# Where the last spectral outputs and the last stores stand in a fused S4D convolution and gated linear unit

## The chip, the cores and the metric

The kernel runs on one core of a Trainium2 chip. The metric is device time in microseconds of one execution; lower is better. Three runs of the kernel before gave 732.49, 735.47 and 735.87 us, median 735.47 us.

The core's engines are named as in the profile: PE (TensorE, matmuls; PEld is its weight load), DVE (VectorE), ACT (ScalarE), POOL (GpSimd) and SP (SyncE). SP, ACT and POOL also issue DMAs; SPq and ACTq are their queues. SBUF and PSUM are on-chip memories of 128 partitions; matmul results land in PSUM.

## The reference

One sequence of 2048 tokens with 448 channels is normalised and goes through two branches, whose sum with the input is the output. Branch A is a long convolution by FFT with a kernel made from state-space parameters, branch B a gated linear unit with 1792 hidden units. All is in float32.

```python
def _A_ref(u, log_A_real, A_imag, C_real, C_imag, log_dt, D_skip):
    ...
    K = 2.0 * jnp.einsum("dn,dnl->dl", C, P).real
    Kf = jnp.fft.rfft(K, L2)
    Uf = jnp.fft.rfft(u_t, L2)
    y = jnp.fft.irfft(Uf * Kf[None, :, :], L2)[:, :, :L]
    ...
    return y + u * D_skip[None, None, :]

def _B_ref(x, w_gate, w_up, w_down):
    g = jnp.einsum("bsd,df->bsf", x, w_gate)
    u = jnp.einsum("bsd,df->bsf", x, w_up)
    h = _sigmoid(g) * u
    return jnp.einsum("bsf,fd->bsd", h, w_down)

xn = _layernorm(x, axis=-1)
return x + _A_ref(xn, ...) + _B_ref(xn, ...)
```

## The kernel before

**Tokens.** The 2048 tokens are 16 blocks of 128. A block's 128 partitions are four groups `g` of 32; four blocks of one tile are four neighbouring tokens, so one partition of a tile [128, 4, 448] holds four rows that are neighbours in DRAM. Four accumulators `accs[0..3]` hold four blocks each. They start as the input x and collect both branches. The first two (blocks 0 to 7) are written to `acc_d` in the middle and come back as the tile `ac`; the last two (blocks 8 to 15) stay in SBUF. Below, `t` is 0 or 1 for `accs[2]` or `accs[3]` and `b` is 0 to 3 for the block in it.

**Two streams of work.** The program is written by two generators, `conv` (branch A) and `glu` (branch B). A planner at the end of the function takes turns between them by the costs that they yield; the order on each engine is then settled by a scheduler, held by `issue_after` (this instruction stands behind that one) and by priorities. The last group of hidden units yields `None` before block (0,1) (L800): from there the planner runs `conv` to its end, and then `glu`.

**The end of `glu`.** For each block the down products (L811) multiply three tiles of hidden units by `w_down`, each as three products of high and low parts, so nine matmuls into one PSUM bank `po`; VectorE adds half of `po` to the accumulator (L816).

**The end of `conv`.** `spectra` goes through the frequencies in 17 steps. In each, `there` (L893) transforms and multiplies, and `back` (L920) makes the inverse's first part into two PSUM banks, which ACT copies to the tile `vt` (L926); four DMAs store `vt` to the DRAM tensor `v_d` (L938), and `turned` (L944) gathers it back transposed into `vp`. `last(h, m)` (L955) makes from `vp` the spectral outputs of channel half `h` for four blocks: 64 matmuls for two calls, and two additions on VectorE for a call (L963). For `m` 0 and 2 these go to `ac`, for 4 and 6 to `accs[2]` and `accs[3]`. `sp_mm`, a one-element list, names the matmul that the following ones must stand behind.

**The stores.** `out(src, b0, h)` (L233 to L240) stores four blocks of one channel half as four DMAs, one for each group, dealt in turn to SP, ACT and POOL by the counter `outs`. `out` of the half `h = 0` of `accs[2]` and `accs[3]` follows their fourth block, that of `h = 1` everything else.

Of the kernel before, what the change touches and what calls it, by code (L numbers as in the profile page):

```python
# [130 lines left out]
def s4d_glu_kernel(ctx, tc, io):  # L131
    nc = tc.nc
# [4 lines left out]
    x_t, out_t = tok(io["A_u"][0]), tok(io["out"][0])  # L137
# [52 lines left out]
    def acc_tile():  # L190
        return pg.tile([128, 4, D], F32, name="acc", bufs=2)
# [37 lines left out]
    accs = [acc_tile() for _ in range(2)]  # L229

    def blocks(t, g, b0, nb):
        return t[g, :, b0 // 8, b0 // 4 % 2, b0 % 4 : b0 % 4 + nb]

    def out(src, b0, h):

        ds = slice(H * h, H * h + H)
        for g in range(4):
            eng = (nc.sync, nc.scalar, nc.gpsimd)[outs[0] % 3]
            outs[0] += 1
            eng.dma_start(blocks(out_t, g, b0, 4)[:, :, ds], src[32 * g : 32 * g + 32, :, ds])  # L240

    def x_load(dst, b0, nb, engs):
        for g in range(4):
            engs[g % len(engs)].dma_start(dst[32 * g : 32 * g + 32], blocks(x_t, g, b0, nb))
# [474 lines left out]
    def glu():  # L719
        for half in range(2):  # L720
# [4 lines left out]
            for fs_ in ORDER[half]:  # L725
# [3 lines left out]
                final = half == 1 and fs_ is ORDER[1][-1]  # L729
# [64 lines left out]
                for t in range(2):  # L794
                    acc = accs[2 * half + t]
                    for b in range(4):
                        if final and (t, b) == (0, 1):

                            yield None
                        if final and (t, b) == (1, 2):  # L800

                            sp_mm[:] = glu_mm
                            for m in (0, 2):
                                lasts[0](1, m)
                        po = psg.tile([128, D], F32, name="po", tag="gu", bufs=4)
                        bs = slice(128 * b, 128 * b + 128)
                        n = 0
                        with tc.issue_after(sp_mm[0].ins) if glu_on else nullcontext():
                            for (hh, hl), (dh, dl) in zip(hs[t], wts):
                                for a_, w_ in ((hh, dh), (hh, dl), (hl, dh)):  # L810
                                    glu_mm[:] = [nc.tensor.matmul(  # L811
                                        po, a_[:, bs], w_, start=(n == 0), stop=(n == 3 * fc - 1)
                                    )]
                                    n += 1
                        with hp(HP):
                            v.scalar_tensor_tensor(  # L816
                                acc[:, b], po, 0.5, acc[:, b], ALU.mult, ALU.add
                            )
                        yield 0.6 * fc
                        if cross and (t, b) in downs:  # L820
                            step(*downs[t, b])
                    if cross:
                        nc.sync.dma_start(acc_d[:, 4 * t : 4 * t + 4], acc)
                    if final:
                        out(acc, 8 + 4 * t, 0)
                if final:
                    sp_mm[:] = glu_mm
                    for m in (4, 6):
                        lasts[0](1, m)
                    for t in range(2):  # L830
                        out(accs[2 + t], 8 + 4 * t, 1)

    def spectra(pf):

# [14 lines left out]
        def work(n, sh, bufs):  # L849
            return spare[n].pop() if spare[n] else pf.tile(sh, F32, name=n, bufs=bufs)  # L850
# [20 lines left out]
        def bank(name):  # L871
            return psc[-1].tile([128, 2, H], F32, name=name, tag="sp", bufs=4)

        def after():
            return tc.issue_after(sp_mm[0].ins)
# [35 lines left out]
        def back(h, k, ys_):  # L911
            vt = work("vt", [128, 2, 2, H], 2)
            bt, n = (t32[:, 1:3], 1) if k == 32 else (bk, 2)
            pvs = [bank("pv") for _ in range(n)]
            with after():
                for j in range(2):
                    for e in range(2):
                        for i in range(n):
                            s = slice(64 * i, 64 * i + 64)
                            mm = nc.tensor.matmul(  # L920
                                pvs[i][:, j], bt[s, e], ys_[j][s, e], start=(e == 0), stop=(e == 1),
                                skip_group_check=True,
                            )
            sp_mm[:] = [mm]
            for i in range(n):
                nc.scalar.copy(vt[:, i], pvs[i])  # L926


            for j in range(2):
                for i in range(n):  # L930
                    k1 = k + 2 * j + i
                    if k == 32:
                        to, fr = v_d[j, 32::64], vt[0:128:2, 0, j]
                    elif k1 == 0:
                        to, fr = v_d[h, 0::64], vt[0:128:2, i, j]
                    else:
                        to, fr = v_d[h, 8 * (k1 % 4) + k1 // 4 :: 32], vt[:, i, j]
                    nc.sync.dma_start(to.rearrange("r w d -> w r d"), fr)  # L938

        def turned(h, k):  # L940
            if h not in vp:
# [4 lines left out]
        def last(h, m):  # L946

            pos = [bank("pv") for _ in range(2)]
            for i in range(2):
                for g in range(4):  # L950
                    for b in range(2):
                        s = slice(64 * b, 64 * b + 64)
                        w = 8 * g + m + i
                        with after():
                            mm = nc.tensor.matmul(  # L955
                                pos[b][32 * g : 32 * g + 32, i], wf[s, w], vp[h][s, w],
                                start=True, stop=True, skip_group_check=True,
                            )
            sp_mm[:] = [mm]
            for b in range(2):  # L960
                q, o, ds = 2 * (m // 4) + b, m % 4, slice(H * h, H * h + H)
                acc = ac[:, 4 * q + o : 4 * q + o + 2, ds] if q < 2 else accs[q][:, o : o + 2, ds]
                v.tensor_tensor(acc, acc, pos[b], ALU.add)  # L963
            if m % 4 == 2 and m < 4:
                for q in range(2):
                    out(ac[:, 4 * q : 4 * q + 4], 4 * q, h)
# [5 lines left out]
        steps = [(h, k) for h in range(2) for k in range(0, 32, 4)]  # L972
# [6 lines left out]
        for n, (h, k) in enumerate(steps):  # L979
# [18 lines left out]
            while len(wait) > 1 and not (due and wait[0][0] == 1):  # L998
                t = wait.pop(0)
# [5 lines left out]
            yield WS  # L1005
        sp_mm[:] = glu_mm
        back(*prev)
        for t in (*wait, prev[:2]):
            turned(*t)
# [92 lines left out]
    lasts, glu_mm, sp_mm, glu_on, outs, x1s, hfs, xls = [], [], [], [], [0], [0], [], []  # L1102
# [7 lines left out]
    while any(g is not None for g in gens):  # L1110
# [3 lines left out]
        i = min(live, key=lambda i: done[i] / total[i])  # L1114
        try:
            w = next(gens[i])
# [31 lines left out]
```

## Time and profile before

| what | value |
|---|---|
| median of three runs | 735.47 us (732.49 to 735.87) |
| the profiled execution | 737.56 us |
| its span, first to last instruction | 735.7 us |
| mean granted TensorE clock | 0.974 |
| DVE, ACT, POOL busy, share of the span | 76%, 57%, 49% |
| HBM read and written | 72.13 MB, 43.84 MB |

A row of the timeline has the start and duration in microseconds, the engine, the line, the operation with output and input, and how many instructions are merged; in brackets stands the idle time of the engine ahead of it and what ended it. The chain of waits follows the last work back through what released each step. A row `min/median/max` gives the duration of one instruction in nanoseconds, and then when the first and the last started. The rows of GB/s show what the DMA engines moved in 40 equal slices of a window.

### The profile page before, as it was taken

What the parts mean: (1) busy time and instruction counts of PE and PEld (TensorE: products, weight loads), DVE (VectorE), ACT (ScalarE), POOL (GpSimd) and SP (SyncE); (2) the same over time, 40 slices, a digit from 0 to 9 for tenths busy, and PEclk for the clock granted to TensorE, in tenths of its full rate; (3) what the DMA queues carried; (4) which work ended last, traced back from release to release, by engine and by line L of the source; (5) the groups of instructions that cost most, each with busy time, mean ns of one, the idle gap of its engine ahead of it and who ended that gap; (6) DMA issues with size and microseconds to landing.
All of it is one profiled execution on the core that took longest, in us unless ns stands there. A gap on an engine that the chain in (4) does not pass through costs nothing.

```text
span 735.7 us, 19244 instructions
## 1 busy us (share of the span) xinstructions
PE 680.4 (92%) x7780; PEld 535.5 (73%) x7780; DVE 560.1 (76%) x776; ACT 421.1 (57%) x654; POOL 360.6 (49%) x423
## 2 busy tenths in 40 slices
PE   2898699999999898899999999999999999989995
PEld 2676588878877787556778878877877777767783
DVE  5899995779889899778488988977955555555543
ACT  3656275479777778796686787677553322312320
POOL 2101076846987975776365697575943002530001
PEclk9998899999999999899999999999999999989998
DMA  9957155454334445456942332233259999997745
GB/s 205 230 147 205 29 165 158 162 172 151 84 111 153 144 118 163 133 151 190 261 141 83 103 109 89 82 112 98 63 162 302 252 243 255 249 263 161 194 120 157
DMA packets 102984, 117.24 MB, mean 159 GB/s; under 512 B 13232, under 2 KB 90864, under 8 KB 102896
## 3 DMA queue, kind: packets, MB, share of 16 engines
q1 hardware_dynamic: 78736, 91.87, 45.2%
q10 hardware_dynamic: 21584, 18.24, 9.3%
q0 software_dynamic: 2576, 5.90, 3.1%
q8 instruction: 61, 1.00, 0.6%
q14 instruction: 27, 0.22, 0.1%
HBM read 72.13 MB, written 43.84 MB: 158 GB/s over the span
## 4 chain that ended last, share of the span: by engine, by line
PE 63%; DVE 13%; DMA 7%; ACT 7%; issue 4%; SPq 3%; POOL 1%; ACTq 1%; POOLq 0%; DVEq 0%
PE gu L698 29%; PE po L811 11%; PE sp L893 7%; PE ko L605 5%; PE pv L920 4%; PE tr L531 3%; DVE Et L591 2%; DVE Ft L593 2%; DVE Et L592 2%; SPq L633 1%; ACT S L540 1%; ACT S L538 1%; DVE acc L816 1%; SPq L481 1%; DMA t<-in_c_t_dram 1%
## 5 line engine op out<-in xcount | busy, mean ns | idle before, releaser
L509 POOL TENSOR_TENSOR me<-me,pm 128x32 f32<-128x32 f32 (+1 forms) x168 | 140.3, 835 | 107.4 <-DVE Et L592 96.3
L509 POOL TENSOR_TENSOR mf<-mf,pm 128x64 f32<-128x64 f32 (+1 forms) x112 | 118.2, 1056 | 4.7
L698 PE MATMUL gu<-xh,wh 128*128 128x512 f32 x336 | 102.3, 412 | 7.0 <-DVE acc L816 6.1
L698 PE MATMUL gu<-xh,wl 128*128 128x512 f32 x336 | 98.9, 402 | 0.0
L698 PE MATMUL gu<-xl,wh 128*128 128x512 f32 x336 | 97.5, 396 | 0.0
L591 DVE TENSOR_TENSOR Et<-me,S 128x1024 f32<-128x1024 f32 x56 | 82.8, 1479 | 12.5 <-ACT S L540 10.8
L592 DVE TENSOR_TENSOR Et<-me,S 128x1024 f32<-128x1024 f32 x56 | 79.4, 1417 | 12.3 <-ACT me L522 9.6
L811 PE MATMUL po<-dh,hh 128*128 128x448 f32 x224 | 85.0, 380 | 3.9 <-DVE hf L709 3.1
L698 PEld LDWEIGHTS gu<-xh,wh 128*128 128x128 f32 x336 | 63.2, 195 | 28.9 <-DVE acc L816 6.5
L811 PE MATMUL po<-dl,hh 128*128 128x448 f32 x224 | 83.0, 371 | 0.0
L811 PE MATMUL po<-dh,hl 128*128 128x448 f32 x224 | 82.0, 369 | 0.0
L537 ACT ACTIVATE S<-tr 128x1024 f32<-128x1024 f32 x56 | 57.8, 1032 | 41.8 <-PE tr L531 41.2
L593 DVE TENSOR_TENSOR Ft<-mf,S 128x1024 f32<-128x1024 f32 x56 | 76.8, 1372 | 5.2 <-ACT S L540 2.7
L605 PEld LDWEIGHTS ko<-Et,Ft 128*32 128x32 f32 x3584 | 54.1, 110 | 32.8 <-issue 13.2
L605 PE MATMUL ko<-Et,Ft 128*32 128x64 f32 x3584 | 65.0, 221 | 12.3 <-DVE Ft L593 11.4
L698 PEld LDWEIGHTS gu<-xh,wl 128*128 128x128 f32 x336 | 65.1, 194 | 15.2 <-DVE pl L316 0.7
L698 PEld LDWEIGHTS gu<-xl,wh 128*128 128x128 f32 x336 | 64.5, 192 | 14.0
L714 ACT CAST hh<-hf 128x512 fp32r<-128x512 f32 x56 | 34.9, 623 | 64.5 <-DVE hf L709 58.6
L709 DVE SCALAR_TENSOR_TENSOR hf<-th,gu 128x512 f32<-128x512 f32 x56 | 38.1, 681 | 43.6 <-PE gu L698 39.5
L706 ACT ACTIVATE th<-gu 128x512 f32<-128x512 f32 x56 | 33.7, 602 | 64.4 <-PE gu L698 52.0
L540 ACT ACTIVATE S<-S,hpi 128x1024 f32<-128x1024 f32 x56 | 65.6, 1171 | 0.5 <-issue 0.3
L816 DVE SCALAR_TENSOR_TENSOR acc<-po,acc 128x448 f32<-128x448 f32 x80 | 48.0, 614 | 21.7 <-PE po L811 21.7
(206 smaller groups left out, 1295.6 us busy)
## 6 DMA issues: line engine op xcount, KB each, us to landing
sk_d<-sk ACTq DMA_DIRECT2D x14, 512.0 KB
sx<-x_d SPq DMA_DIRECT2D x32, 224.0 KB
skl<-sk_d SPq DMA_DIRECT2D x16, 448.0 KB
vp<-v_d SPq DMA_DIRECT2D x16, 448.0 KB
v_d<-vt SPq DMA_DIRECT2D x62, 112.0 KB
ph<-ph_d SPq DMA_DIRECT2D x224, 24.0 KB
wt_d<-wh SPq DMA_DIRECT2D x9, 512.0 KB
wt_d<-wl SPq DMA_DIRECT2D x9, 512.0 KB
```

Of the source, the lines that this page charges most:

```text
L509: ins = nc.gpsimd.tensor_tensor(m[:, :, w + a : 2 * w : n], m[:, :, a:w:n], par(base + i).unsqueeze(2).to_broadcast([128, 4 * DC, w // n]) ...
L537: nc.scalar.activation(rows(cs), pv, AF.Abs)
L540: sins[:] = [nc.scalar.activation(cs, cs, AF.Sin, scale=-TWO_PI, bias=hpi)]
L591: v.tensor_tensor(Et[:, :, :, 32:64], two(me[:, :, 32:64]), S[:, 1::-1], ALU.mult)
L592: v.tensor_tensor(Et[:, :, :, 0:32], two(me[:, :, 0:32]), S[:, 1:3, :, ::-1], ALU.mult)
L593: fts[:] = [v.tensor_tensor(Ft, two(mf), S[:, 3:5], ALU.mult)]
L605: mm = nc.tensor.matmul(ko[32 * j : 32 * j + 32, sl], Ft[:, cc, DC * h + 4 * q + j], Et[:, cc, DC * h + 4 * q + j], start=(k == 0), stop=( ...
L698: glu_mm[:] = [nc.tensor.matmul(ps, a_, b_, start=(n == 0), stop=(n == len(mm) - 1))]
L709: marks[1] = v.scalar_tensor_tensor(hf, th, 1.0, pgu[1], ALU.add, ALU.mult)
L811: glu_mm[:] = [nc.tensor.matmul(po, a_[:, bs], w_, start=(n == 0), stop=(n == 3 * fc - 1))]
L816: v.scalar_tensor_tensor(acc[:, b], po, 0.5, acc[:, b], ALU.mult, ALU.add)
L893: mm = nc.tensor.matmul(to, tb[:kk, t, 64 * c : 64 * c + 64], rhs, start=True, stop=True, skip_group_check=True,)
```

## The change

Three things are edited. The two calls `last(1, 0)` and `last(1, 2)` stand ahead of block (1,1) in place of (1,2), and `last(1, 4)` and `last(1, 6)` ahead of block (1,2) in place of behind everything. The stores of the last blocks are regrouped: half 1 of `accs[2]` and whole rows of blocks 0 and 1 of `accs[3]` follow `last(1, 6)`, and blocks 2 and 3 of `accs[3]` are stored as whole rows, each behind its own addition; a new function `rest` does this. Of the last step's four stores of `vt`, the two with `i == 1` are issued by ACT.

```diff
+    def rest(src, b0, b, nb):
+
+        for g in range(4):
+            eng = (nc.sync, nc.scalar, nc.gpsimd)[outs[0] % 3]
+            outs[0] += 1
+            eng.dma_start(blocks(out_t, g, b0 + b, nb), src[32 * g : 32 * g + 32, b : b + nb])
...
-                        if final and (t, b) == (1, 2):
+                        if final and t == 1 and b in (1, 2):
 
                             sp_mm[:] = glu_mm
-                            for m in (0, 2):
+                            for m in (4 * b - 4, 4 * b - 2):
                                 lasts[0](1, m)
+                            if b == 2:
+                                out(accs[2], 8, 1)
+                                rest(accs[3], 12, 0, 2)
...
+                        if final and t == 1 and b >= 2:
+                            rest(acc, 12, b, 1)
...
-                    if final:
-                        out(acc, 8 + 4 * t, 0)
-                if final:
-                    sp_mm[:] = glu_mm
-                    for m in (4, 6):
-                        lasts[0](1, m)
-                    for t in range(2):
-                        out(accs[2 + t], 8 + 4 * t, 1)
+                    if final and t == 0:
+                        out(acc, 8, 0)
...
-                    nc.sync.dma_start(to.rearrange("r w d -> w r d"), fr)
+                    eng = nc.scalar if i == 1 and (h, k) == steps[-1] else nc.sync
+                    eng.dma_start(to.rearrange("r w d -> w r d"), fr)
```

The file grows by seven lines ahead of the change, so L698, L811, L816, L920, L938, L944, L955 and L963 become L705, L821, L826, L926, L945, L951, L962 and L970.

VectorE's last instructions, which follow the order of the matmuls on PE, before (`acc_4170` is `accs[2]`, `acc_4175` is `accs[3]`, `ac_6953` is `ac`; `po` are down products, `pv` spectral outputs):

```order
L816 SCALAR_TENSOR_TENSOR acc_4175<-po_8568,acc_4175 128x448
L816 SCALAR_TENSOR_TENSOR acc_4175<-po_8579,acc_4175 128x448
L963 TENSOR_TENSOR ac_6953<-ac_6953,pv_8590 128x2x224
L963 TENSOR_TENSOR ac_6953<-ac_6953,pv_8591 128x2x224
L963 TENSOR_TENSOR ac_6953<-ac_6953,pv_8610 128x2x224
L963 TENSOR_TENSOR ac_6953<-ac_6953,pv_8611 128x2x224
L816 SCALAR_TENSOR_TENSOR acc_4175<-po_8638,acc_4175 128x448
L816 SCALAR_TENSOR_TENSOR acc_4175<-po_8649,acc_4175 128x448
L963 TENSOR_TENSOR acc_4170<-acc_4170,pv_8664 128x2x224
L963 TENSOR_TENSOR acc_4175<-acc_4175,pv_8665 128x2x224
L963 TENSOR_TENSOR acc_4170<-acc_4170,pv_8684 128x2x224
L963 TENSOR_TENSOR acc_4175<-acc_4175,pv_8685 128x2x224
```

and with the change:

```order
L826 SCALAR_TENSOR_TENSOR acc_4175<-po_8568,acc_4175 128x448
L970 TENSOR_TENSOR ac_6953<-ac_6953,pv_8579 128x2x224
L970 TENSOR_TENSOR ac_6953<-ac_6953,pv_8580 128x2x224
L970 TENSOR_TENSOR ac_6953<-ac_6953,pv_8599 128x2x224
L970 TENSOR_TENSOR ac_6953<-ac_6953,pv_8600 128x2x224
L826 SCALAR_TENSOR_TENSOR acc_4175<-po_8627,acc_4175 128x448
L970 TENSOR_TENSOR acc_4170<-acc_4170,pv_8638 128x2x224
L970 TENSOR_TENSOR acc_4175<-acc_4175,pv_8639 128x2x224
L970 TENSOR_TENSOR acc_4170<-acc_4170,pv_8658 128x2x224
L970 TENSOR_TENSOR acc_4175<-acc_4175,pv_8659 128x2x224
L826 SCALAR_TENSOR_TENSOR acc_4175<-po_8686,acc_4175 128x448
L826 SCALAR_TENSOR_TENSOR acc_4175<-po_8701,acc_4175 128x448
```

One block stands between the two groups of spectral additions, and two stand behind them.

The end of SP's queue before, from the last stores of `vt` on:

```order
L938 DMA v_d_62<-vt_8511 32x4x224 x4
L944 DMA vp_8161<-v_d_62 16x32x224
L240 DMA out_0_dram<-acc_4170 32x4x224
L240 DMA out_0_dram<-ac_6953 32x4x224 x3
L240 DMA out_0_dram<-acc_4175 32x4x224
L240 DMA out_0_dram<-acc_4170 32x4x224 x2
L240 DMA out_0_dram<-acc_4175 32x4x224
```

and with the change:

```order
L945 DMA v_d_62<-vt_8511 32x4x224 x2
L951 DMA vp_8161<-v_d_62 16x32x224
L240 DMA out_0_dram<-acc_4170 32x4x224
L240 DMA out_0_dram<-ac_6953 32x4x224 x3
L247 DMA out_0_dram<-acc_4175 32x896 x2
L240 DMA out_0_dram<-acc_4170 32x4x224
L247 DMA out_0_dram<-acc_4175 32x448 x2
```

SP issues two stores fewer ahead of the gather, and its last two stores are single blocks.

The end of ACT with the change:

```order
L932 COPY vt_8511<-pv_8512 128x448
L932 COPY vt_8511<-pv_8513 128x448
L945 DMA v_d_62<-vt_8511 32x4x224 x2
L240 DMA out_0_dram<-acc_4170 32x4x224
L240 DMA out_0_dram<-ac_6953 32x4x224 x3
L247 DMA out_0_dram<-acc_4175 32x896
L240 DMA out_0_dram<-acc_4170 32x4x224
L247 DMA out_0_dram<-acc_4175 32x448 x3
```

The other two stores of `vt` stand behind the two copies that make it and ahead of all output stores; POOL's last three stores are single blocks as well, the last two of them of block 3. Ahead of these places the order on every engine is as before, and no wait is added to the matmuls of `last`.

## The prediction

> **What bounds the kernel now.** The change touches only the end, so I read the page for the whole, then the chain of waits, then the last 30 us engine by engine.
>
> ```profile
> span 735.7 us, 19244 instructions
> PE 680.4 (92%) x7780; PEld 535.5 (73%) x7780; DVE 560.1 (76%) x776; ACT 421.1 (57%) x654; POOL 360.6 (49%) x423
> ```
>
> TensorE (PE) is busy 92% of the span and its work is the same after the change, so what can move is where it waits and what follows its last matmul. The chain of waits over the end (start, duration, what):
>
> ```profile
> 709.76 5.79 PE po L811 x27
> 716.22 3.10 DMA out_dram<-acc
> 719.42 1.75 PE pv L955 x64
> 721.17 3.86 PE po L811 x18
> 725.03 0.02 issue
> 725.05 0.64 DVE acc L816
> 725.69 0.28 issue
> 725.97 0.47 POOL out_dram L240
> ...
> 728.00 0.55 POOL out_dram L240
> ```
>
> The piece at 716.22 carries a store's name, but it ends where PE begins the spectral outputs (`last`, L955), which need the gather `vp`; the timelines of PE and of the queues SP, ACT and POOL place it:
>
> ```profile
> 717.23 0.37 PE L811 MATMUL po<-dh,hh 128*128 128x448 f32 x1
> 719.42 1.75 PE L955 MATMUL pv<-vp,wf 64*32 64x224 f32 x64 [0.18 <-DMA out_dram<-acc]
> 724.94 1.74 PE L955 MATMUL pv<-vp,wf 64*32 64x224 f32 x64
> ...
> 707.69 0.58 SPq L944 DMA_DIRECT2D vp<-v_d  x1
> 710.35 2.46 SPq L938 DMA_DIRECT2D v_d<-vt  x4
> 714.39 0.58 SPq L944 DMA_DIRECT2D vp<-v_d  x1
> 716.22 0.35 SPq L240 DMA_DIRECT2D out_dram<-acc  x1
> 722.20 1.44 SPq L240 DMA_DIRECT2D out_dram<-ac  x3
> 725.70 3.60 SPq L240 DMA_DIRECT2D out_dram<-acc  x4
> ...
> 709.79 0.97 ACT L926 COPY vt<-pv 128x448 f32<-128x448 f32 x2 [3.89 <-PE pv L920]
> ...
> 728.00 1.10 POOL L240 DMA_DIRECT2D out_dram<-acc  x2 [0.94 <-DVE acc L963]
> ```
>
> Two things close the kernel. First a round trip through DRAM: the vt copies end at 710.76, four v_d stores go out on SP, the gather follows at 714.39, and PE may start `last` at 719.42. Five blocks of down products cover the trip so well that PE stands only 0.18 us. Then the drain: PE ends at 726.68, VectorE still adds the spectral halves to 728.23, and the stores follow:
>
> ```profile
> 720.49 2.21 DVE L963 TENSOR_TENSOR ac<-ac,pv 128x448 f32<-128x448 f32 x4 [0.58 <-PE pv L955]
> 725.05 0.62 DVE L816 SCALAR_TENSOR_TENSOR acc<-po,acc 128x448 f32<-128x448 f32 x1 [1.19 <-PE po L811]
> 726.02 2.21 DVE L963 TENSOR_TENSOR acc<-acc,pv 128x448 f32<-128x448 f32 x4 [0.35 <-PE pv L955]
> ```
>
> The DMA traffic in slices of 0.5 us, from 706 and from 716:
>
> ```profile
> GB/s 198 217 13 0 0 0 116 201 342 163 90 233 190 151 135 215 0 0 0 47 149 335 240 203 289 330 217 27 0 33 0 0 0 0 174 174 170 373 303 290
> GB/s 149 335 240 203 289 330 217 27 0 33 0 0 0 0 174 174 170 373 303 290 299 203 242 242 206 176 283 181 305 280 289 303 84 13 0 0 0 16 0 0
> ```
>
> The second line's last big slices end at 732.5, a remnant follows to 733.0; I take 732.75. From there to the end of the span (735.7) are 2.95 us in which nothing moves but 16 GB/s in one slice; I leave them as they are.
>
> **The change part by part.** *The filler that leaves.* `last(1, 0)` and `last(1, 2)` move ahead of block (1,1), so PE reaches them at 717.23, where that block began, not at 719.4. Unless the gather is ready 2.19 us sooner, PE now stands where it worked.
>
> *The gather.* Two of the four v_d stores go to ACT's queue, behind the two vt copies and with nothing of ACT's waiting behind them but the first output store, at 716.22. One issue costs:
>
> ```profile
> L938 SPq DMA_DIRECT2D v_d<-vt x8: 525/602/603, 703.4 to 712.2; - x8
> ```
>
> The last of the four starts at 712.2 now. With the change SP issues two from 710.35 and ACT two from 710.76, so the last starts at 710.76 + 0.60 = 711.36, 0.84 sooner, and the gather at 714.39 - 0.84 = 713.55. The gather before it, undisturbed, was issued at 707.69 and filled the slices from 709.0 to a little past 711.0: its 448 KB had moved 3.3 to 3.8 us after issue. The last gather started its bytes at 715.5 but shared the slices from 717.5 on with the stores issued at 716.22 and released PE 5.03 us after issue. Issued at 713.55 it has moved by 716.9 to 717.4, ahead of most of these. Behind the bytes comes the signal: the v_d bytes end in the slice to 714.0, and the gather that waits for them went out at 714.39, so I add 0.4. That gives 717.3 to 717.8; I take **717.5**, PE idle 0.3 in place of 0.18. The bounds are 717.23 (PE is not there sooner) and 719.42 (nothing gained).
>
> *PE and VectorE behind it.* From the gather on PE has its 1.75, one block at half of 3.86 = 1.93, the other spectral outputs 1.75, then two blocks 3.86: 9.29. The second outputs reuse PSUM banks that the first four additions free; these begin 1.07 after PE starts `last` and take 2.21, done at 3.28, and PE comes for the banks at 3.68: no wait. VectorE ends with one addition, 0.02 + 0.64: 9.95 in all, against 8.81 before (728.23 - 719.42). So **727.45** in place of 728.23. The other four additions end 2 us ahead of PE's last block and lie beside it.
>
> *The stores.* Block 3's four stores of 56 KB go to SP, ACT and twice POOL. POOL starts 0.28 after VectorE's addition in the chain and takes 0.55 an issue, so its second starts at 727.45 + 0.28 + 0.55 = 728.28. For how long a store then takes the trace has those of 112 KB on POOL (second row; the first is SP's issues):
>
> ```profile
> L240 SPq DMA_DIRECT2D out_dram<-acc x4: 316/379/670, 725.7 to 728.6; - x4
> ...
> DMA to landing us min/median/max: 2.8/3.5/4.1
> ```
>
> The long ones lie behind 448 KB pieces still moving; here the pieces ahead are smaller and issued earlier, so I take the shortest, 2.8: **731.1** in place of 732.75. Whole rows of 1,792 bytes replace halves; I count nothing for it. The load ahead does not hold this up: five outputs of 448 KB moved from 723.0 to 732.75, and the same bytes started 1.92 sooner and as slow would be through at 730.85. Nor does issuing: SP and ACT hold five stores each from 723.4 on (717.5 + 3.68 + 1.07 + half of 2.21), at up to 0.67 us (SP's row above; its four in 3.60 include waits), done before 727.45 but for the last. For the cost of a small store the ends are 2.6 (2.8 less half of 112 KB at 250 GB/s) and 3.5.
>
> The Trainium skill, "DMA: Bandwidth & Descriptors", section "Rules for kernel authors", speaks against single blocks: under 64 KB one pays mostly overhead; its section "Anatomy of one DMA — SWDGE (gpsimd) path" fits 2.0 us plus bytes over 436 GB/s, an estimate of 2.13 us for 56 KB. By it the bytes would be there at 730.4 and the span 733.4; the trace's shortest, 2.8 us for 112 KB where the fit gives 2.26, is longer, so the row stands.
>
> *Sum.* 732.75 - 731.1 = 1.65 us off the profiled span of 735.7, so 734.05. That execution took 737.56 in all, and the runs have a median of 735.47; I take the same 1.65 off: **733.8**. With 717.23 and 2.6 the gain is 2.1, with 717.8 and 3.5 it is 0.65.
>
> **The rivals.** *The gather comes no sooner.* If the v_d bytes and not their issue set its start, or if the out stores at 716.22 still collide with it, PE stands from 717.23 to 719.42 and everything behind is 1.92 later than my sum: bytes at 733.0 with 2.8, at 733.7 with 3.5. That is 0.25 to 0.95 slower, 735.7 to 736.4. It decides from a gather landing at 719.15 on (717.5 + 1.65). For it: during the v_d stores the traffic is 135 to 233 GB/s, and the sum has no slack at 717.23. Against it: other slices reach 373, so four stores spaced 0.60 apart are held by their issue.
>
> The Trainium skill has this rival's rule in the same page, section "Issuing engines are not separate DMA queues": all queues end on the same 16 engines, and another one saves only the issuing time, usually small beside the transfer. That the saving here is just issuing time, 0.84 us of it, the spacing of 602 ns bears out.
>
> *A gain that can be told from none.* About 0.5% (3.7 us) is what a measurement of this kernel can tell from no change. The end holds no such gain: 2.19 at the gather is given back but for 0.78, and the drain cannot go below the 2.6. But the runs shown reach from 732.49 to 735.87; should the low ones be the usual ones for the new program, the median is 732.49 - 1.65 = 730.8.
>
> *The end is no chain but a stream.* If the stores move at the old mean, 730.85 instead of 731.1 comes out; at the worst slices (176 to 206 GB/s) the 1.4 MB behind the first spectral outputs, whose bytes start about 724.2 (723.4 and the 0.8 from 722.20 to 723.0), take 7.2 and end at 731.4. Both stay within my bounds.
>
> **How the numbers follow.** Forecast with its stream variant (733.4 to 734.8): 0.60. Gather no sooner (735.7 to 736.4): 0.14. The low end of the executions (730.8 to 731.8): 0.20. Something slower that no row shows, such as a gather after 722.8, 739 and more: 0.06. Faster by over 0.5% (below 731.8) is the third case, slower the fourth, no change the other two: 0.20, 0.74, 0.06. The range takes the forecast, the late gather and half of the low executions: 731.3 to 736.2.
>
> **What would show it.** In the new profile: the two ACT stores of v_d start near 710.8, the gather is issued near 713.6, PE starts L962 near 717.5 with an idle time under 0.6 put down to a DMA, the last VectorE addition ends near 727.5, and traffic stops near 731.1, 2.95 before the end. A gather issued after 714.2, a PE gap over 1.5 us, or traffic beyond 732 would make me wrong, and so would a difference ahead of 700 us, where no engine's order changes.

## The result and the profile after

The changed kernel has a median of 735.0 us over 22 runs (731.17 to 738.88), the kernel before, run beside it on the same chips, 735.62 us over 22 (730.57 to 740.11). The ratio on record is 1.0002 (that of the two medians is 0.9992) with a 95% interval from 0.9982 to 1.0022: no change that can be told. The forecast of 1.65 us, a ratio of 0.9978, lies just below that interval.

The profiled execution of the changed kernel took 735.32 us. The head of its page, to be held against that of before (735.7 us):

```profile
span 733.5 us, 19250 instructions
```

The span is 2.2 us shorter, and that would look like the forecast come true. It is not. No engine's order differs ahead of the last `back`, so its start on PE is a fair zero for both executions. Before, in the timeline, followed by a wait of PE 54 us earlier:

```profile
707.97 1.78 PE L920 MATMUL pv<-yy,bk 64*128 64x224 f32 x16
...
653.38 1.72 PE L955 MATMUL pv<-vp,wf 64*32 64x224 f32 x16 [2.67 <-DVE pd L905]
```

and after:

```profile
706.00 1.78 PE L926 MATMUL pv<-yy,bk 64*128 64x224 f32 x16
...
654.53 0.96 PE L962 MATMUL pv<-vp,wf 64*32 64x224 f32 x16 [2.09 <-DVE pd L911]
```

The lead of 1.97 us is there before the first changed instruction runs. It comes from one place. When the waits shown end, the execution before is still 1.15 us ahead (653.38 against 654.53). The windows of 653.00 to 660.20 us (length, busy time of PE, PEld, DVE, ACT and POOL, then granted clock, DMA share, GB/s) in the execution before

```profile
653.00:660.20 7.20, 6.82 (x29) 4.75 (x30) 2.96 (x7) 0.07 (x1) 2.81 (x4) 0.53 1.05 274
```

and after

```profile
653.00:660.20 7.20, 5.67 (x37) 4.45 (x38) 4.12 (x9) 0.60 (x1) 3.05 (x6) 1.00 1.04 275
```

show PE at a granted clock of 0.53 in one and 1.00 in the other, behind waits of 2.67 and 2.09 us for the same thing. At the ninth row of matmuls after those, the execution before is 1.93 us behind (661.57 against 659.64 us), nearly the whole 1.97. No order differs there, so I take it for chance between executions and not for the edit. So the end is read from the start of `back`.

The chain of waits of the changed kernel, its last 19 us:

```profile
714.25 2.71 DMA out_dram<-acc
...
716.97 1.75 PE pv L962 x64
718.72 2.01 PE po L821 x9
720.74 1.67 PE pv L962 x64
722.41 3.85 PE po L821 x18
...
726.28 0.64 DVE acc L826
...
727.19 0.51 POOL out_dram L247
```

PE's order is the intended one: outputs, one block, outputs, two blocks. The piece at 714.25 again carries a store's name and ends where the gather lets PE go. The rows of the timeline that place the rest, PE and SP's queue, and then the issues of `vt`'s stores on ACT (min/median/max in ns, first and last start):

```profile
716.97 1.75 PE L962 MATMUL pv<-vp,wf 64*32 64x224 f32 x64 [1.56 <-DMA out_dram<-acc]
...
711.84 0.58 SPq L951 DMA_DIRECT2D vp<-v_d  x1
...
L945 ACTq DMA_DIRECT2D v_d<-vt x2: 584/601/618, 708.8 to 709.4; - x2
```

The traffic in slices of 0.5 us from 714:

```profile
GB/s 346 197 181 256 325 246 75 33 0 0 0 0 0 154 181 145 382 292 298 341 351 258 229 190 264 298 296 262 294 287 68 0 0 0 0 16 0 0 0 0
```

Bytes end near 729.4. Counted from the start of the last `back` (subtract 707.97 before and in the forecast, 706.00 after), in us:

| step | before | forecast | after |
|---|---|---|---|
| last store of `vt` starts to issue | 4.2 | 3.4 | 3.4 |
| gather issued | 6.42 | 5.58 | 5.84 |
| first spectral outputs on PE | 11.45 | 9.53 | 10.97 |
| PE's wait ahead of them | 0.18 | 0.3 | 1.56 |
| last addition on VectorE ends | 20.26 | 19.48 | 20.92 |
| last bytes | 24.8 | 23.1 | 23.4 |
| end of the span | 27.73 | 26.08 | 27.5 |

The changed end is 0.2 us shorter, not 1.65. Outputs start 0.48 sooner, the longer chain behind them costs 1.14, the stores give back 2.0 between addition and last bytes, and the stretch without traffic, 2.95 before, takes 1.15 more. (The last two are one shift, seen from the last bytes; the part on why the prediction was right or wrong takes it up.)

### The profile page after: what moved, and what is told of

It reads as the page before. It is cut to its first block, busy times and chain, and to the rows that moved or that the text cites. A ratio compares the mean times of both kernels' runs of the same rounds, so it can differ in the third digit from the quotient of the medians.

```text
span 733.5 us, 19250 instructions
## 1 busy us (share of the span) xinstructions
PE 677.8 (92%) x7780; PEld 533.6 (73%) x7780; DVE 557.4 (76%) x776; ACT 421.6 (57%) x654; POOL 364.2 (50%) x425
## 4 chain that ended last, share of the span: by engine, by line
PE 67%; DVE 11%; DMA 7%; issue 4%; ACT 3%; SPq 3%; POOL 3%; ACTq 1%; POOLq 0%; DVEq 0%
PE gu L705 29%; PE po L821 14%; PE sp L899 7%; PE ko L612 6%; PE pv L926 4%; PE tr L538 4%; DVE Ft L600 2%; DVE Et L599 1%; DVE pm L452 1%; DMA t<-in_c_t_dram 1%; SPq L640 1%; DVE Et L598 1%; SPq L488 1%; DMA ph<-ph_d 1%; DVE pl L329 1%
## 5 line engine op out<-in xcount | busy, mean ns | idle before, releaser
L516 POOL TENSOR_TENSOR mf<-mf,pm 128x64 f32<-128x64 f32 (+1 forms) x112 | 121.6, 1086 | 4.7
L705 PE MATMUL gu<-xh,wh 128*128 128x512 f32 x336 | 100.3, 406 | 6.8 <-DVE acc L826 6.1
L705 PE MATMUL gu<-xh,wl 128*128 128x512 f32 x336 | 96.9, 395 | 0.0
L705 PE MATMUL gu<-xl,wh 128*128 128x512 f32 x336 | 96.4, 392 | 0.0
L821 PE MATMUL po<-dh,hh 128*128 128x448 f32 x224 | 86.2, 385 | 5.4 <-DVE hf L716 3.1
L821 PE MATMUL po<-dl,hh 128*128 128x448 f32 x224 | 83.9, 375 | 0.0
L821 PE MATMUL po<-dh,hl 128*128 128x448 f32 x224 | 83.0, 374 | 0.0
L705 PEld LDWEIGHTS gu<-xh,wh 128*128 128x128 f32 x336 | 62.0, 191 | 27.1 <-DVE acc L826 6.5
L600 DVE TENSOR_TENSOR Ft<-mf,S 128x1024 f32<-128x1024 f32 x56 | 75.1, 1342 | 5.9 <-POOL me L516 1.8
L705 PEld LDWEIGHTS gu<-xh,wl 128*128 128x128 f32 x336 | 63.8, 190 | 14.7 <-DVE pl L323 0.7
L705 PEld LDWEIGHTS gu<-xl,wh 128*128 128x128 f32 x336 | 63.4, 189 | 13.4
L826 DVE SCALAR_TENSOR_TENSOR acc<-po,acc 128x448 f32<-128x448 f32 x80 | 48.3, 616 | 20.4 <-PE po L821 20.3
```

Source lines behind the costliest of these rows:

```text
L516: ins = nc.gpsimd.tensor_tensor(m[:, :, w + a : 2 * w : n], m[:, :, a:w:n], par(base + i).unsqueeze(2).to_broadcast([128, 4 * DC, w // n]) ...
L600: fts[:] = [v.tensor_tensor(Ft, two(mf), S[:, 3:5], ALU.mult)]
L705: glu_mm[:] = [nc.tensor.matmul(ps, a_, b_, start=(n == 0), stop=(n == len(mm) - 1))]
L821: glu_mm[:] = [nc.tensor.matmul(po, a_[:, bs], w_, start=(n == 0), stop=(n == 3 * fc - 1))]
L826: v.scalar_tensor_tensor(acc[:, b], po, 0.5, acc[:, b], ALU.mult, ALU.add)
```

## The experiments

One run of the kernel before beside the first seven of these took 737.47 us. All ends below are counted from the start of the last `back`, so that what an execution won or lost earlier doesn't enter.

**Two queues alone.** The kernel before, with the stores of `vt` on two queues and nothing else.

```diff
-                    nc.sync.dma_start(to.rearrange("r w d -> w r d"), fr)
+                    eng = nc.scalar if i == 1 and (h, k) == steps[-1] else nc.sync
+                    eng.dma_start(to.rearrange("r w d -> w r d"), fr)
```

> The order of before, with the last step's two i == 1 stores of vt issued by ACT and nothing else changed. All numbers count from the start of the last back on PE (before: gather issued at 6.42, last spectral outputs start at 11.45 after 0.18 idle, span ends at 27.69). Theory A, the issue on SP holds the gather: it goes out near 5.84 as in the changed kernel, its signal comes 4.9 to 5.1 later at 10.7 to 11.0, but PE is at its filler until 11.27, so the idle time goes to 0.0 and the span ends 0.2 sooner, near 27.5. Rival B, the v_d bytes and not their issue set the gather: issue at 6.4, idle 0.18, end 27.7. Neither predicts a total that can be told from before.

734.07 us, span 732.3. Rows of its timeline, PE and SP's queue:

```profile
705.26 1.78 PE L920 MATMUL pv<-yy,bk 64*128 64x224 f32 x16
716.46 1.74 PE L956 MATMUL pv<-vp,wf 64*32 64x224 f32 x64
...
711.26 0.58 SPq L945 DMA_DIRECT2D vp<-v_d  x1
```

The gather goes out at 6.00 instead of 6.42, and the outputs start at 11.20 with no idle time in brackets: PE still had blocks to do. The end is at 27.0, 0.7 under before, where 27.5 was expected. The saving at the issue is there, 0.42 us; how much of the 0.7 is owed to it isn't shown, since the outputs start only 0.25 sooner.

**The order alone.** The changed kernel with all four stores of `vt` on SP.

```diff
-                    eng = nc.scalar if i == 1 and (h, k) == steps[-1] else nc.sync
-                    eng.dma_start(to.rearrange("r w d -> w r d"), fr)
+                    nc.sync.dma_start(to.rearrange("r w d -> w r d"), fr)
```

> The changed kernel with all four stores of vt on SP as before: the new order alone. Counted from the start of the last back (changed kernel: gather issued at 5.84, spectral outputs start at 10.97 after 1.56 idle, last addition done at 20.92, end 27.53). Theory A, the gather takes 4.8 to 5.1 from issue whatever lies beside it: issue at 6.4, spectral outputs at 11.4 to 11.5 with 2.0 to 2.1 idle on PE, last addition at 21.4, end 28.0. Rival B, the gather's length of 5 us comes from the output stores that it meets, so a later gather meets more of them: outputs later than 11.7 and end after 28.3. Rival C, the drain is a stream that does not care: end at 27.5.

736.84 us, span 734.9. In the timeline:

```profile
705.36 1.78 PE L926 MATMUL pv<-yy,bk 64*128 64x224 f32 x16
716.72 2.43 PE L961 MATMUL pv<-vp,wf 64*32 64x224 f32 x64 [1.94 <-DMA out_dram<-acc]
...
727.68 0.62 DVE L826 SCALAR_TENSOR_TENSOR acc<-po,acc 128x448 f32<-128x448 f32 x1 [1.23 <-PE po L821]
...
711.78 0.58 SPq L950 DMA_DIRECT2D vp<-v_d  x1
```

The gather is issued at 6.42 and outputs start at 11.36, after a wait of 1.94: near theory A, and against rival B, which had them later than 11.7. But the end is at 29.5, where A had 28.0, and the outputs took 2.43 us for 1.75. The windows behind the wait say why; the first number after the busy times is the granted clock:

```profile
716.70:718.00 1.30, 1.28 (x48) 1.27 (x56) 0.22 (x1) 0.00 (x0) 0.00 (x0) 0.86 0.18 51
...
721.00:722.00 1.00, 1.00 (x7) 0.64 (x6) 0.00 (x0) 0.00 (x0) 0.18 (x1) 0.97 0.89 161
```

Between these two the clock is 0.50 throughout. If it is half wherever it isn't full, the mean of 0.86 puts the start at 717.64 and that of 0.97 the finish at 721.06: 3.4 us, which by this estimate cost 1.7 of work, on top of the gap's own 1.94.

**The order alone, with PE kept at work.** The same, with nine matmuls on old data put into the gap.

```diff
+                        if final and (t, b) == (1, 1):
+                            warm = psg.tile([128, D], F32, name="po", tag="gu", bufs=4)
+                            with tc.issue_after(glu_mm[0].ins):
+                                for j in range(9):
+                                    glu_mm[:] = [nc.tensor.matmul(
+                                        warm, hs[1][0][0][:, 128:256], wts[0][0], start=(j == 0), stop=(j == 8)
+                                    )]
+                            v.tensor_copy(junk[:, 0:1], warm[:, 0:1])
```

> The order-only kernel (all four vt stores on SP) plus nine matmuls with one repeated operand pair into a spare PSUM bank between block (1,0) and the first spectral outputs, and one copy of a column of it on VectorE; their result is used nowhere. Counted from the start of the last back; the order-only kernel had spectral outputs at 11.36 after 1.94 idle, half clock from 12.3 to 15.7, last addition at 22.95, end 29.59. Theory G, the idle time on PE brought the half clock down: the filler takes 1.9 of the gap, outputs start at 11.3 to 11.4 after 0.0 to 0.3 idle, full clock throughout, last addition at 21.3 to 21.4, end 27.9 to 28.2. Rival H, the half clock came for another reason (the rate of the whole stretch, or chance) or the slow stretch was contention with the stores: last addition at 22.5 or later, end 29 or later.

735.12 us, span 733.3:

```profile
705.43 1.78 PE L934 MATMUL pv<-yy,bk 64*128 64x224 f32 x16
716.75 1.75 PE L969 MATMUL pv<-vp,wf 64*32 64x224 f32 x64
726.07 0.62 DVE L834 SCALAR_TENSOR_TENSOR acc<-po,acc 128x448 f32<-128x448 f32 x1 [1.19 <-PE po L829]
```

Outputs start at 11.32, as late as without the filler, but take 1.75, and the last addition begins 20.64 behind `back` instead of 22.32. The end is at 27.9, as the theory of the clock had it: 1.7 us of the 29.5 were the half clock. It is one execution of each; the last section shows on what else the clock depends.

**The changed kernel again.** For the spread of its end, and to see whether its own gap halves the clock.

> The changed kernel once more, unaltered, to see how far its end repeats when the rest of the execution differs. Counted from the start of the last back: if the end is a chain of fixed pieces, gather issued at 5.8 to 6.0, spectral outputs at 10.8 to 11.0 after 1.4 to 1.6 idle on PE, last addition at 20.8 to 21.0, end 27.2 to 27.9, whatever the span. If the clock gate can also catch this kernel's idle of 1.6, a half clock shows in the stretch behind the gather and the last addition comes 1.5 or more later, end above 29.

733.43 us, span 731.4:

```profile
704.14 1.78 PE L926 MATMUL pv<-yy,bk 64*128 64x224 f32 x16
714.77 1.75 PE L962 MATMUL pv<-vp,wf 64*32 64x224 f32 x64 [1.22 <-DMA out_dram<-acc]
```

The outputs start at 10.63, the wait is 1.22 (both a little under what was expected), the outputs keep 1.75, and the end is at 27.3, beside 27.5 in the first profile. Ends of one kernel differ by a few tenths, so what the two queues and the order bring apart from each other can't be ranked.

**The last stores off POOL.** The stores of blocks 2 and 3 go to SP and ACT in turn.

```diff
-            eng = (nc.sync, nc.scalar, nc.gpsimd)[outs[0] % 3]
+            eng = (nc.sync, nc.scalar)[g % 2] if nb == 1 else (nc.sync, nc.scalar, nc.gpsimd)[outs[0] % 3]
```

> The changed kernel with the eight single-block stores of block 2 and 3 on SP and ACT in turn, none on POOL. Counted from the start of the last back (changed kernel: last addition at 20.92, last bytes at 23.4, end 27.53, so 4.1 us of closing where before had 2.9). Theory D, the closing waits for POOL, which ends some 2.3 us behind the landing of its own last store: POOL's last store is now one issued 3.4 us sooner, the closing goes back below 3 us and the end comes to 25.9 to 26.5. Rival E, the closing is a fixed time behind the last store of any queue: end 27.3 to 27.6. Rival F, SP and ACT with four single-block stores each are slower to issue than three queues: last bytes later than 23.8 and end after 27.7.

733.3 us, span 730.8. The timeline, then the window behind the last bytes:

```profile
704.89 1.78 PE L926 MATMUL pv<-yy,bk 64*128 64x224 f32 x16
715.75 1.75 PE L962 MATMUL pv<-vp,wf 64*32 64x224 f32 x64 [1.44 <-DMA out_dram<-acc]
725.06 0.62 DVE L826 SCALAR_TENSOR_TENSOR acc<-po,acc 128x448 f32<-128x448 f32 x1 [1.19 <-PE po L821]
```

```profile
728.50:730.80 2.30, 0.00 (x0) 0.00 (x0) 0.00 (x0) 0.00 (x0) 0.00 (x0) 0.76 0.01 4
```

Up to the last bytes little changed: the last addition begins at 20.17 (20.28 in the changed kernel) and bytes end some 2.3 us before the end, at 23.6 (23.4). The end is at 25.9, 1.6 sooner, within what the theory of POOL's closing gave. That is all in the stretch without traffic, 4.1 us with POOL and 2.3 without.

**One block later.** Both pairs of spectral outputs move behind one more block, which fills PE's gap; one block follows them instead of two.

```diff
-                        if final and t == 1 and b in (1, 2):
+                        if final and t == 1 and b in (2, 3):
...
-                            for m in (4 * b - 4, 4 * b - 2):
+                            for m in (4 * b - 8, 4 * b - 6):
...
-                            if b == 2:
-                                out(accs[2], 8, 1)
-                                rest(accs[3], 12, 0, 2)
+                            if b == 3:
+                                out(accs[2], 8, 1)
+                                rest(accs[3], 12, 0, 3)
...
-                        if final and t == 1 and b >= 2:
+                        if final and t == 1 and b == 3:
```

> The changed kernel with each pair of spectral outputs one block later: the first ahead of block (1,2), the second ahead of block (1,3), then the stores of accs[2] half 1 and of blocks 0 to 2 of accs[3] in whole rows, and block 3's behind its addition. Counted from the start of the last back. PE works through block (1,1) until 11.27, the gather is there at 11.0, so PE does not stand. The PE and VectorE work from there is 8.1 and the last addition ends at 19.35 where the changed kernel has 20.92. Theory A, the end is a chain through the last addition: end 1.3 to 1.6 sooner than the changed kernel, 25.9 to 26.3. Rival C, the end is the stream of 2.3 MB of stores behind the first spectral outputs at 260 to 290 GB/s: the first of them start 0.3 later and the end is 27.4 to 28.1.

734.59 us, span 732.8. Timeline, traffic from 714, and the landing of POOL's last two stores:

```profile
704.54 1.78 PE L926 MATMUL pv<-yy,bk 64*128 64x224 f32 x16
715.75 1.74 PE L962 MATMUL pv<-vp,wf 64*32 64x224 f32 x64
723.23 0.62 DVE L826 SCALAR_TENSOR_TENSOR acc<-po,acc 128x448 f32<-128x448 f32 x1 [0.50 <-PE po L821]
...
723.57 1.09 POOL L247 DMA_DIRECT2D out_dram<-acc  x2
...
GB/s 224 326 276 100 0 33 0 0 0 0 39 201 152 242 323 350 290 239 161 251 221 287 167 190 260 344 271 237 215 126 25 0 0 0 16 0 0 0 0 0
...
DMA to landing us min/median/max: 5.7/5.7/5.7
```

PE doesn't wait, and the last addition ends at 19.31, as worked out and 1.6 before the changed kernel's. Yet bytes flow until 729.4, at 24.9, and the end is at 28.3: later, against the chain theory and a little beyond its rival's 27.4 to 28.1. From 719.5 to 729.4 the queues never run dry. Here the stores end the kernel and not the sums: POOL's last two land 5.7 us behind their issue, and the bytes take 10 us, where those of the changed kernel took 9 (from 720.5). Whether their sum holds them up, or the larger stores of 168 KB on each queue, isn't separated. So filling PE's gap this way wins nothing; what is left to try is to have the outputs themselves sooner.

**The gather in parts.** The version off POOL, with the last gather in eight parts of 56 KB, on SP and ACT in turn. Each part holds every eighth of the 32 columns that the matmuls of `last` take.

```diff
             s = slice(k // 4, 128, 8)
+            if (h, k) == steps[-1]:
+                for w in range(8):
+                    eng = (nc.sync, nc.scalar)[w % 2]
+                    eng.dma_start(vp[h][s, w::8], v_d[h, s, w::8])
+                return
             nc.sync.dma_start(vp[h][s], v_d[h, s])
```

> The kernel with the last stores off POOL, and the last gather split into eight of 56 KB by the rows that each pair of spectral outputs needs, in turn on SP and ACT, so that last(1, 0) waits for the first two only. Counted from the start of the last back; the kernel that it builds on had the gather issued at 5.93, outputs at 10.86, last addition at 20.80, end 25.93. If the gather's 4.9 us are mostly its bytes and their order, the first parts land 3.4 to 3.9 after issue, outputs start at 9.5 to 10.1, the last addition ends at 19.4 to 20.1 and the span at 24.6 to 25.4. Rival, a gather takes 4.7 us whatever its size (fixed latency): outputs at 10.7 or later, end 25.8 or later.

732.81 us, span 730.8:

```profile
706.77 1.78 PE L926 MATMUL pv<-yy,bk 64*128 64x224 f32 x16
716.12 1.74 PE L967 MATMUL pv<-vp,wf 64*32 64x224 f32 x64
725.42 0.62 DVE L826 SCALAR_TENSOR_TENSOR acc<-po,acc 128x448 f32<-128x448 f32 x1 [1.20 <-PE po L821]
...
712.68 2.50 SPq L954 DMA_DIRECT2D vp<-v_d  x4
```

The first parts go out at 5.91 and PE takes the outputs at 9.35 with no wait, 1.6 sooner than the changed kernel; 3.44 us after the first issue instead of 5.13. The last addition ends at 19.27 and the span at 24.0, better than the expected 24.6 to 25.4.

**The parts alone.** The same gather in the changed kernel, with POOL's stores kept.

> The changed kernel with the last gather in parts and POOL kept for the last stores. If the two savings add, the spectral outputs start at 9.2 to 9.5 after the start of the last back, the last addition ends at 19.2 to 19.4, and the end is 25.4 to 26.0 (23.98 and the 1.6 of POOL's closing). If the stores of this earlier end are held by their stream, the last bytes do not follow and the end is above 26.5.

735.46 us, span 733.7:

```profile
707.77 1.78 PE L926 MATMUL pv<-yy,bk 64*128 64x224 f32 x16
717.11 1.74 PE L967 MATMUL pv<-vp,wf 64*32 64x224 f32 x64
```

Outputs at 9.34, end at 25.9, as expected. The two edits add up: 27.3 to 27.5 becomes 25.9 with either (1.4 to 1.6 us) and 24.0 with both. The single time of this run is no better than before, since `back` began as late as in the execution before; only the end shows the edit.

**Timings.** The version off POOL and the one with parts as well, in five rounds each.

> The changed kernel with only its eight single-block stores taken off POOL, timed. Its end was 25.93 us, 1.76 less than before's: ratio 0.9976 if ends are all that differs, which the interval of about 0.003 to each side can not tell from 1. Its end in this profile again 25.6 to 26.2; above 27 the first one was chance and not POOL.

> The kernel with the last gather in parts and the last stores off POOL, now timed against before. Its end was 23.98 us long from the start of the last back, before's 27.69: 3.7 less, 0.50% of 735.6. If the ends are all that differs between the programs, the ratio comes out at 0.995 with an interval that reaches about 0.003 to each side, since executions of one program differ by 2 us and more through stretches of half clock elsewhere; the end in this profile again 23.7 to 24.3. If a shorter end is paid back elsewhere, or the total is set by other things, the ratio is 0.998 or above.

> The kernel with the last gather in parts and the last stores off POOL, timed a second time, since its end is 3.7 us shorter than before's in both profiles but the first timing gave a ratio of 0.998 with an interval from 0.9954 to 1.0006. If the shorter end is what it is worth, 0.995, the new ratio lies between 0.992 and 0.998; if the total gets back some of it elsewhere, at or above 0.998 again. The end in the profile: 23.9 to 24.1 from the start of the last back.

| kernel | median us | before, same chip | ratio, 95% interval | end behind `back` |
|---|---|---|---|---|
| off POOL | 732.36 | 734.38 | 0.9972, 0.9944 to 1.0 | 25.4 |
| off POOL, gather in parts | 731.74 | 734.38 | 0.998, 0.9954 to 1.0006 | 24.0 |
| the same again | 730.16 | 734.8 | 0.9936, 0.9913 to 0.9958 | 24.1 |

The ratios are those on record and not quotients of the two medians (in the second row that would be 0.9964). The end off POOL, 25.4, is a little under the expected 25.6 to 26.2. By the ends, 27.7 against 24.0, the version with parts should be 3.7 us faster, a ratio of 0.995. Its two timings lie on either side, and only the second is clear of no change. It is the best version found; how much it wins is settled no better than some tenths of a per cent.

## Why the prediction was right and where it was wrong

The verdict, no change that can be told, was right, and with it the median of 735.0, but that says little for the working behind it: the 22 runs of one kernel span 7.7 to 9.5 us, and a gain of 0.2 us and one of 1.65 hardly differ beside that. The forecast behind it was 1.65 us sooner; the trace shows 0.2. One step, the time of the gather, accounts for nearly all of the difference. Step by step:

**The two queues: right at the issue, a little less behind it.** The last store of `vt` starts 0.83 sooner, as the sum had it (0.84). The gather follows it by 2.4 us instead of 2.19, so that 0.6 of this is left. The Trainium skill, "DMA: Bandwidth & Descriptors", section "Issuing engines are not separate DMA queues", gave that limit, only issuing time to be saved; the trace agrees with its 0.83, and returns 0.2 of it.

**The gather: the term that was mis-sized.** "Issued at 713.55 it has moved by 716.9 to 717.4", plus 0.4 for the signal, gave 3.95 us from issue to PE. Measured are 5.13 in the changed kernel and 4.94 with the order alone, beside 5.03 before. The prediction had the 5.03 in its own row and explained away over 1 us of it as sharing with the output stores, taking instead the time in which an earlier gather's bytes passed through the slices. That was the wrong choice: the time from issue to the consumer's start is a measured whole, while the slices don't say which transfer's bytes they hold, nor when the consumer is let go. Hence outputs at 10.97 instead of 9.53, and PE's wait of 1.56 instead of 0.3; the prediction had set a gap of over 1.5 us as what would prove it wrong.

So the first rival, the gather no sooner, was half right: its rule (PE stands where it worked) is what happened, though the outputs did come 0.48 sooner. Whether the 5 us are the gather's own or still owed to the stores that start 2.4 us behind it (714.25 in the chain) was not separated in full: in six profiles in which PE waited for the whole gather it took 4.88 to 5.13 us, with stores that start 1.8 to 2.6 us behind it and no trend between the two, but no run takes the stores away. In parts PE had no wait 3.44 us after the first issue; whether a part ends sooner or only the first matmuls no longer wait for the whole isn't told apart either.

**PE and VectorE behind the gather: right.** 9.95 us from outputs to the end of the last addition were forecast, and 9.95 are in the rows (716.97 to 726.28 + 0.64).

**The small stores: as forecast, by another measure.** The prediction took a time from issue to landing, 2.8 us, for the time to the last bytes. The landing of POOL's last two stores, in the kernel before (112 KB each) and in the changed one (56 KB each):

```profile
DMA to landing us min/median/max: 4.1/4.1/4.1
...
DMA to landing us min/median/max: 2.6/2.7/2.9
```

Before, the second of them started at 728.55 and landed at 732.65, 0.1 ahead of the last bytes of all queues. After, it started at 727.70 and landed at 730.3 to 730.6, about 1 us behind the last bytes. From the end of the addition to that landing are 3.4 to 3.7 us, where 3.65 were forecast; to the last bytes it is 2.5, and 4.5 before.

The shortest landing, 2.6, is the lower bound that the prediction gave. The Trainium skill, "DMA: Bandwidth & Descriptors", section "Anatomy of one DMA — SWDGE (gpsimd) path", puts 2.13 us on 56 KB as an estimate from its fit; the 2.6 is longer, and the measurement stands.

**The closing: a constant counted from the wrong event.** "From there to the end of the span (735.7) are 2.95 us in which nothing moves but 16 GB/s in one slice; I leave them as they are." Counted so, from the last bytes, it took 4.1. Counted from the landing of POOL's last store it is 3.05 before and 2.9 to 3.2 after, so the 2.95 holds behind a landing; that landing and last bytes fell together in the profile before was luck. With "one block later" that store's issue began about 724.1 (half of 1.09 behind 723.57) and landed 5.7 later, at 729.8, and the span ended 3.0 behind that. That the queue decides is shown: the same bytes on SP and ACT closed in 2.3 us. What POOL does in those 3 us has a name in the trace. Instructions of the name DRAIN at the program's end, in the changed kernel and then off POOL (min/median/max in ns, first and last start; the longest on POOL is the first):

```profile
L1151 POOLq DRAIN  x3: 46/93/5145, 727.6 to 733.3; - x3
L1151 SPq DRAIN  x3: 7/7/39, 731.2 to 733.0; - x3
...
L1151 POOLq DRAIN  x3: 46/102/6727, 722.9 to 730.5; - x3
L1151 SPq DRAIN  x3: 7/7/7, 730.0 to 730.3; - x3
```

In the changed kernel POOL's DRAIN lasts until 732.8, when SP has long come to its own, at 731.2; off POOL it is over at 729.6, ahead of SP's 730.0. The span ends 0.7 to 0.8 behind the later of the two. In ten profiles read for it, POOL's DRAIN ended 2.2 to 2.8 us behind the landing of POOL's own last store. Why it takes that long is open.

**The stream: next bound, and not fully told apart.** In the changed kernel POOL's last two stores landed 2.6 and 2.9 us behind their issue, near the 2.3 to 2.7 of the other profiles that keep this order and POOL's stores; one block later they took 5.7. So the chain through the last addition decided the changed kernel's end, and the stores did one block later. The last bytes can be put down to either: the traffic of the changed kernel, too, keeps to 262 to 298 GB/s for the last 3 us up to 729.0.

**What was gained and given back**, then: 1.44 us of the forecast went to the gather, which leaves 0.2 of 1.65. The forecast's own sum with the measured gather gives an end of 26.08 + 1.44 = 27.52, and 27.5 was measured. Read by the last bytes, 1.15 went to the closing and 1.15 came back from the small stores, which is one shift, of the last bytes against the landing, counted once each way. Two slips in the working change nothing: 732.75 less 1.92 is 730.83 and not 730.85, and the last slice above 100 GB/s in its second row ends at 732.0 and not at 732.5 (slices of 0.1 us have the last bytes at 732.8). The half clock was in no part of the prediction; the changed kernel's two profiles escaped it at the end, and whether other executions of it did isn't known.

**The other signs and cases.** A difference ahead of 700 us was named as a sign against the prediction, and there is one, of 1.97 us; it stands where no order differs, and the second profile of the same kernel moved by 1.86 again. The case that the low executions become the usual ones didn't happen: the 22 runs of the kernel before have nearly the median that the first three had (735.62 and 735.47), and those of the changed kernel lie among them.

## What to carry to other kernels

Work taken out of the shadow of a round trip must be weighed against the time from issue to the consumer's start in the trace, whole, and not against the part of it in which bytes are seen moving. Where PE waits for one large gather, cut it so that the first matmuls need only its first part. And look at which queue the very last store is on: here the end came about 3 us behind the landing of POOL's last store, and two other queues for the same bytes were worth 1.4 to 2.1 us.

## What the runs showed of the hardware

**A wait of about 2 us can halve PE's clock; where it falls decides.** Waits of 1.22, 1.26, 1.44, 1.56 and 2.09 us left the clock at 1.00, one of 1.94 was followed by 3.4 us at 0.50, and one of 2.67 by a granted clock of 0.53 over 7.2 us (at half where not full: 6.8 us). So length alone doesn't decide. The starts of the half clock fall on a grid: in the changed kernel's profile, worked out from windows of 1 us, they are at 124.34, 329.14 and 728.50 us among others, which are 60 and 117 times 3.413 us apart. Windows cut on the grid of each profile (PE's busy time comes second, the granted clock third from the end), of the kernel before, of the changed one, and of the order alone:

```profile
649.76:653.17 3.41, 0.95 (x29) 0.39 (x12) 3.41 (x4) 0.00 (x0) 2.74 (x2) 1.00 1.07 318
...
649.99:653.41 3.42, 2.45 (x58) 1.43 (x54) 3.38 (x5) 0.53 (x1) 3.04 (x3) 1.00 1.11 277
653.41:656.82 3.41, 2.29 (x22) 1.66 (x23) 3.41 (x8) 0.00 (x0) 0.54 (x1) 1.00 1.01 268
714.85:718.26 3.41, 1.85 (x59) 1.48 (x65) 0.84 (x2) 0.00 (x0) 0.76 (x2) 1.00 0.71 171
...
714.23:717.64 3.41, 1.47 (x43) 1.10 (x49) 0.62 (x1) 0.00 (x0) 0.74 (x2) 1.00 0.82 212
717.64:721.06 3.42, 3.42 (x44) 2.49 (x25) 2.30 (x4) 0.00 (x0) 0.97 (x2) 0.50 0.12 27
```

The half clock followed the windows in which PE was busy for 0.95 and 1.47 us. The wait of 2.09 is split by an edge of the grid at 653.41, so that both windows keep more work, and that of 1.56 leaves 1.85 in its window. Between 100 and 723 us of all thirteen profiles, each of the 21 windows at full clock with PE busy under 49% was followed by half clock, 5 of 15 between 49% and 55%, and 6 of 2,269 above, which this doesn't explain. The Trainium skill, "TensorE: Matmul & The Clock Gate", Part 1, tells of a window of about 3.4 us that runs freely, and of half clock after an idle one; the grid agrees with both the length and the free running. That an idle time has to fill the window doesn't agree: 1.94 us was enough.

**Executions of one program differ by more than this change.** The changed kernel's 22 runs span 7.7 us, and the last `back` began at 706.00 and 704.14 in two profiles of it. A change of 1 to 3 us at the end is seen when time is counted from a matmul ahead of it, and hardly in the medians.
